# In the first batch, a layer-one tile is copied out of PSUM behind its own last matmul

## The chip, the cores and the metric

The kernel runs on one core of one Trainium2 chip. The metric is the device time of one execution in microseconds (us). Before the change it is 1329.47 us, the median of three runs (1329.26 to 1331.39).

## The reference, cut to what matters

```python
# q, k, v: (8 batches, 8 heads, 576 rows, 64); tau: a scalar
scores = (q @ k.T) / sqrt(64)
keep   = scores >= max(scores, axis=-1) - tau
attn   = exp(scores - max) where keep, else 0;  attn /= sum(attn) + 1e-9
x = (attn @ v) with heads side by side            # (4608 tokens, 512)
h = x @ w_in                                      # (4608, 2048)   "layer one"
out = (0.5 * h * (1 + erf(h / sqrt(2)))) @ w_out  # exact GELU, then "layer two": (4608, 512)
```

All of it is float32. The two weight matrices arrive as 64-bit floats and are turned into float32 on the chip, in pieces of 512 columns (lines L199 and L200 on ScalarE, L207 and L208 on VectorE, L219 on GpSimd).

## The kernel before, in words

The order of the instructions is written out by hand: each engine runs its queue in the order in which the Python code emits it. No scheduler moves anything.

**Slots.** The main loop at the end of the function runs over slots `n`. A slot is one chunk of 128 score rows of one pair of heads (for the last 64 rows of both heads together, the tail chunk). The first batch, `early`, is slots 0 to 19: chunks 0 and 1 of the four pairs in slots 0 to 7, then chunks 2, 3 and tail of each pair in turn in slots 8 to 19. `BATCH` is 20, the first slot of the second batch.

**One early slot** emits, in this order:

1. `scores`: matmuls into the PSUM tiles `sc` (L403; two buffers), and `softmax_head`: the negated row maximum `nmx` on VectorE (L415), a threshold on GpSimd (L418), and the exponential `p` on ScalarE (L420).
2. `gelus(0)`: every finished layer-one tile still in the list `late` is copied out of PSUM by ScalarE (`g<-hT`, L641). In the first batch the GELU itself is put off (`hold`), so that the ScalarE table of the exponential stays loaded. The eight copies wait in the list `held` until `gelus_held()` at slot 20.
3. In every third slot, `weigh_v`: the weights times v into a PSUM tile `xT` (L574), copied out by ScalarE (L592).
4. In the slots with a long transposed part, the first half of the weight conversion on ScalarE (L199, L200).
5. `fill`: matmuls of layer one of block 0 (L674), six or seven calls in a slot, from slot 10 on. Eight calls (two groups of four) make one tile `hT`, so that 64 calls make the eight tiles of the block. One call shows as two rows in the trace.
6. `turn_p_early`: PE transposes of the previous slot's `p` into PSUM tiles `tr` (L347), copied out by ScalarE (`pT<-tr`, L354, L357, L362, L366).
7. `softmax_tail`: VectorE masks `p` and sums it (L436). This is the last reader of `sc`.
8. The rest of the weight conversion (L199 and L200 on ScalarE, L207 and L208 on VectorE; L219 on GpSimd follows in the next slot).

**PSUM.** `hT`, `tr`, `xT` and a few others share one pool with the tag `mm` and four buffers. A new tile takes the buffer that was given back longest ago in program order, and its first matmul waits until the last reader of the old tile is done.

**SBUF scratch.** The copies `g` and the conversion's scratch `power` share a pool of ten buffers.

**Names that follow.** T1 to T8 are the eight layer-one tiles of block 0. Counting six or seven calls a slot from slot 10, the last matmul of T1 is the first call of slot 11's fill, that of T2 the third of slot 12's, T3 the fourth of slot 13's, T4 the sixth and last of slot 14's, T5 the first of slot 16's, T6 the third of slot 17's, T7 the fourth of slot 18's, T8 the sixth and last of slot 19's.

From slot 20 on, `lag[0]` is set anew in every slot (2, at the very end 0), so that the value in the diff is used in the first batch alone.

Of the kernel before, what the change touches and what calls it, by code (L numbers as in the profile page):

```python
# [18 lines left out]
def kernel(  # L19
# [606 lines left out]
    BLK_NS = N_DF * (N_DM * NS_IN + TOK // P * NS_OUT)  # L626

    late = []
    lag = [1]
    dirty = [False]  # L630
    held = []
    hold = [True]
# [665 lines left out]
```

## Time and profile before

| | us |
|---|---|
| median of three runs | 1329.47 |
| the profiled execution, its own time | 1329.71 |
| its span, first to last instruction | 1327.7 |
| PE busy in the span | 1315.7 |
| DVE, POOL, ACT busy | 1040.3, 637.1, 604.9 |

PE is TensorE's matmul queue, PEld its weight loads, DVE VectorE, ACT ScalarE, POOL GpSimd. Times in the timeline count from the start of the span. A timeline row gives start, duration, engine, line, operation, output and inputs, how many instructions are merged, and in brackets how long the engine had been idle and what released it. The slots that matter here begin with these scores (L403) on PE:

| slot | 11 | 12 | 13 | 14 | 15 | 16 | 17 | 18 | 19 | 20 |
|---|---|---|---|---|---|---|---|---|---|---|
| scores start, us | 62.4 | 68.2 | 77.4 | 82.7 | 87.5 | 96.3 | 101.5 | 106.7 | 115.3 | 121.0 |
| fill starts, us | 64.4 | 73.0 | 78.3 | 83.9 | 92.3 | 97.1 | 102.6 | 111.3 | 116.2 | none |
| transposes start, us | 66.9 | 75.9 | 80.9 | 86.3 | 95.2 | 99.7 | 105.5 | 113.7 | 118.8 | none |

### The profile page before, as it was taken

The page shows a single profiled execution, that of the slowest core. Times are in us where ns is not written, and L with a number is a line of the kernel's source. Part 1 is how long each engine was busy: PE and PEld are TensorE (multiplying, and loading weights), DVE is VectorE, ACT ScalarE, POOL GpSimd, SP SyncE. Part 2 cuts the span into 40 slices and gives each one's busy share as a digit, 9 for nine tenths or more (in the row PEclk, how much of TensorE's full clock was granted, in tenths as well). Part 3 has the DMA queues.
Part 4 walks back from the last instruction along what each step waited for, and adds up shares of the span by engine and source line. Part 5 has one row for each costly group of instructions (what it writes and reads, how often), then busy time and mean ns, then how long its engine had stood idle before and what let it go on. Part 6 is the DMA issues. An engine that isn't in the chain of part 4 may idle for free.

```text
span 1327.7 us, 19863 instructions
## 1 busy us (share of the span) xinstructions
PE 1315.7 (99%) x6306; PEld 889.1 (67%) x6306; DVE 1040.3 (78%) x2001; ACT 604.9 (46%) x1027; POOL 637.1 (48%) x1058
## 2 busy tenths in 40 slices
PE   9999999999999999999999999999999999999998
PEld 6776466576476466466466466578778787877877
DVE  6887877888888888888888888883857698386674
ACT  7988366376376368358458438232111203211120
POOL 3565545455555555655555541236264403645430
PEclk9999999999999999999999999999999999999999
DMA  7553667777776787787787775400000140000003
GB/s 250 180 177 89 143 156 164 168 161 161 190 167 157 191 185 160 191 194 164 185 202 159 177 172 110 105 9 1 1 0 1 40 107 14 0 1 0 1 0 80
DMA packets 213687, 153.14 MB, mean 115 GB/s; under 512 B 117264, under 2 KB 196992, under 8 KB 213584
## 3 DMA queue, kind: packets, MB, share of 16 engines
q1 hardware_dynamic: 195440, 125.31, 40.6%
q0 software_dynamic: 17712, 26.26, 7.4%
q8 instruction: 52, 0.85, 0.3%
q14 instruction: 51, 0.42, 0.1%
q10 hardware_dynamic: 432, 0.30, 0.1%
HBM read 56.62 MB, written 12.58 MB: 52 GB/s over the span
## 4 chain that ended last, share of the span: by engine, by line
PE 92%; ACT 2%; DVE 2%; DMA 1%; issue 1%; POOL 1%; SPq 0%; DVEq 0%; POOLq 0%; ACTq 0%
PE bank L862 34%; PE o_ps L689 17%; PE hT L674 16%; PE sc L403 13%; PE xT L574 11%; ACT p L420 1%; DVE nmx L415 1%; DMA inv<-turned 0%; PE tr L347 0%; ACT pT L354 0%; DVE p L436 0%; DVE power L208 0%; DVE power L207 0%; DMA xall<-in_moe_w_out_dram 0%; DMA turned_p<-in_moe_w_out_dram 0%
## 5 line engine op out<-in xcount | busy, mean ns | idle before, releaser
L420 ACT ACTIVATE p<-sc,nmx 128x576 f32<-128x576 f32 x288 | 202.0, 738 | 277.9 <-DVE nmx L415 277.6
L436 DVE SCALAR_TENSOR_TENSOR p<-sc,thr,p 128x576 f32<-128x576 f32 x288 | 225.4, 816 | 72.7 <-ACT p L420 65.2
L418 POOL TENSOR_SCALAR thr<-nmx,tau_eff 128x1 f32<-128x1 f32 x288 | 84.7, 296 | 335.1 <-DVE nmx L415 332.5
L674 PE MATMUL hT<-xall,w_in 128*128 128x256 f32 x1024 | 241.8, 385 | 0.0
L415 DVE TENSOR_REDUCE nmx<-sc 128x1 f32<-128x576 f32 x288 | 205.2, 749 | 44.3 <-PE sc L403 43.0
L689 PE MATMUL o_ps<-w_out,g 128*128 128x512 f32 x512 | 236.7, 602 | 0.0
L674 PEld LDWEIGHTS hT<-xall,w_in 128*128 128x128 f32 x1024 | 189.4, 190 | 51.3 <-issue 24.5
L744 DVE TENSOR_TENSOR o<-o,bank 128x256 f32<-128x256 f32 (+1 forms) x242 | 100.0, 417 | 94.5 <-PE bank L862 89.5
L744 DVE TENSOR_TENSOR c<-c,bank 128x320 f32<-128x320 f32 x304 | 146.7, 487 | 34.3 <-PE bank L862 21.1
L689 PEld LDWEIGHTS o_ps<-w_out,g 128*128 128x128 f32 x512 | 93.1, 190 | 109.6 <-issue 106.8
L403 PE MATMUL sc<-kT,qT 64*128 64x288 f32 x960 | 161.3, 429 | 2.1 <-DVE p L436 1.2
L574 PE MATMUL xT<-pT,v 128*64 128x320 f32 (+1 forms) x1240 | 159.3, 409 | 0.2
L535 DVE STREAM_TRANSPOSE turned_p<-p 128x1152 f32<-128x1152 f32 x112 | 154.4, 1378 | 3.9
L403 PEld LDWEIGHTS sc<-kT,qT 64*128 64x128 f32 x960 | 91.8, 186 | 77.0 <-issue 61.9
L574 PEld LDWEIGHTS xT<-pT,v 128*64 128x64 f32 x1240 | 86.4, 137 | 70.9 <-issue 10.4
L862 PE MATMUL bank<-w_out,c 128*128 128x256 f32 (+1 forms) x484 | 120.5, 379 | 0.8 <-DVE o L744 0.8
L260 POOL DMA_DIRECT2D v<-in_v_dram x208 | 111.2, 538 | 3.4 <-issue 1.2
L862 PEld LDWEIGHTS bank<-w_out,c 128*128 128x128 f32 x484 | 90.3, 190 | 18.9 <-DVE o L744 3.2
L929 ACT ACTIVATE c<-c 128x320 f32<-128x320 f32 (+1 forms) x80 | 46.9, 624 | 114.7 <-DVE c L744 114.6
L744 POOL TENSOR_TENSOR c<-c,g 128x320 f32<-128x320 f32 (+1 forms) x40 | 50.6, 1273 | 67.4 <-DVE c L744 67.4
L862 PE MATMUL bank<-t_out,g 128*128 128x256 f32 (+1 forms) x324 | 82.4, 377 | 0.4 <-DVE o L744 0.4
L862 PE MATMUL bank<-t_out,c 128*128 128x256 f32 x320 | 82.8, 381 | 0.0
(185 smaller groups left out, 1749.1 us busy)
## 6 DMA issues: line engine op xcount, KB each, us to landing
pT<-turned_p SPq DMA_DIRECT2D x448, 160.0 KB, 3.6
pT<-pd_tail SPq DMA_DIRECT2D x112, 80.0 KB, 3.0
q<-in_q_dram POOLq DMA_DIRECT2D x104, 72.0 KB, 3.6
k<-in_k_dram POOLq DMA_DIRECT2D x104, 72.0 KB, 3.2
inv<-turned SPq DMA_DIRECT2D x54, 128.0 KB, 4.0
v<-in_v_dram POOLq DMA_DIRECT2D x156, 40.0 KB, 3.1
out_dram<-o SPq DMA_DIRECT2D x40, 128.0 KB, 2.4
xall<-in_moe_w_out_dram SPq DMA_DIRECT2D x9, 512.0 KB, 4.9
```

Source lines behind the costliest of these rows:

```text
L260: eng.dma_start(t[r:P:4, e, 0:n, :], rows[:, r * KR:r * KR + n, :])
L403: nc.tensor.matmul(sc[e][:, h, 0:HALF], lhsT=lhsT, rhs=s["kT"][rows, at:at + HALF], start=True, stop=True)
L415: nc.vector.tensor_reduce(nmx[:, e:e + 1], sc, axis=AXIS.XY, op=ALU.max, negate=True)
L418: nc.gpsimd.tensor_scalar(thr[:, e:e + 1], nmx[:, e:e + 1], -1.0, tau_eff, op0=ALU.mult, op1=ALU.subtract)
L420: nc.scalar.activation(w[:, e * S:(e + 1) * S].rearrange("p (h s) -> p h s", h=2), sc, AF.Exp, bias=nmx[:, e:e + 1], scale=1.0)
L436: nc.vector.scalar_tensor_tensor(row, sc[e][:, :, 0:HALF], thr[:, e:e + 1], row, op0=ALU.is_ge, op1=ALU.mult, accum_out=den[e])
L535: nc.vector.transpose(turned_p[:, :, i // 2, 0:NB, i % 2 * Q:(i % 2 + 1) * Q], w.rearrange("p (e b i) -> p e b i", e=2, i=Q))
L574: nc.tensor.matmul(to, lhsT=s["v"][:, e, c, :], rhs=rhs, start=(c == 0), stop=(c == KR - 1))
L674: nc.tensor.matmul(hT[:, j % 2, :], lhsT=w_in_sb[c][:, j * P:(j + 1) * P], rhs=x_blk[n][:, c, :], start=(c == 0), stop=(c == N_DM - 1))
L689: nc.tensor.matmul(o[:, 0:d_model], lhsT=g[j][:, m * P:(m + 1) * P], rhs=w_out_sb[j], start=(j == 0), stop=(j == N_DF - 1))
L744: eng.tensor_tensor(out, a, b, op=ALU.add)
L862: nc.tensor.matmul(to, lhsT=l, rhs=r, start=start and k == 0, stop=k == len(pairs) - 1, skip_group_check=not start)
```

## The change

`lag[0]` is how many finished layer-one tiles `gelus` leaves in `late` when it is called from inside `block_steps`, right behind the last matmul of a tile. With 1, a finished tile stays in PSUM until the next one is finished or until the next slot calls `gelus(0)`. With 0, its ScalarE copy is emitted at once: ahead of the same slot's transposes and their copies.

```diff
@@ -626,7 +626,7 @@
     late = []
-    lag = [1]
+    lag = [0]
     dirty = [False]
```

In the built program the instructions of PE, DVE, POOL and SP stand in the same order as before. On ACT the eight `g<-hT` copies stand earlier, each by one slot or less; nothing else moves. The tiles' buffers turn over in another order with it.

## The prediction

> **What bounds the kernel now.** I read the chain of work that ended last first, then the busy times by stretch, then the waits inside the first batch, then its timeline. The chain:
>
> ```profile
> PE 92%; ACT 2%; DVE 2%; DMA 1%; issue 1%; POOL 1%; SPq 0%; DVEq 0%; POOLq 0%; ACTq 0%
> ```
>
> PE carries the end, so only what moves PE counts. Busy time by stretch, slots 10 to 20 (57 to 127 us) and after them; the columns are the length, then PE, PEld, DVE, ACT, POOL busy:
>
> ```profile
> 57.00:127.00 70.00, 67.82 (x372) 48.72 (x372) 57.36 (x113) 58.95 (x119) 40.04 (x59) 1.00 0.49 144
> 127.00:179.00 52.00, 51.92 (x198) 27.08 (x198) 41.50 (x78) 19.68 (x34) 28.47 (x57) 1.00 0.65 145
> ```
>
> In the first batch PE has 2.2 us of gaps, ACT is at 84%, DVE at 82%: three engines hand work round. Afterwards PE has no gap to speak of, so a shift of PE at 127 us should go through to the end. The waits from 57 to 127 us (sum, times, longest):
>
> ```profile
> ACT pT L354 <- PE tr L347: 5.7, 5, 1.6
> DVE nmx L415 <- PE sc L403: 5.4, 4, 2.2
> ...
> PEld tr L347 <- ACT pT L354: 2.4, 5, 0.5
> ...
> PE sc L403 <- DVE p L436: 0.7, 2, 0.5
> ...
> PEld tr L347 <- ACT g L641: 0.3, 1, 0.3
> ```
>
> PE's own wait is that of the transposes for a PSUM buffer: 2.4 + 0.3 us. Slot 12 shows one (timeline):
>
> ```profile
> 72.97 2.89 PEld L674 LDWEIGHTS hT<-xall,w_in 128*128 128x128 f32 x14 [0.49 <-issue]
> ...
> 72.99 0.58 ACT L641 COPY g<-hT 128x512 f32<-128x512 f32 x1
> ...
> 75.89 1.01 PEld L347 LDWEIGHTS tr<-ident,p 128*128 128x128 f32 x8
> ...
> 76.79 1.07 ACT L354 COPY pT<-tr 128x512 f32<-128x512 f32 x2 [0.54 <-PE tr L347]
> 77.43 0.14 PEld L347 LDWEIGHTS tr<-ident,p 128*128 128x128 f32 x1 [0.53 <-ACT pT L354]
> ...
> 77.60 1.14 PE L403 MATMUL sc<-kT,q_tail 128*128 128x288 f32 x4
> ```
>
> Eight transposes run, the ninth waits 0.53 us until ACT has emptied the first `tr` tile: of the four buffers a finished tile (T2) and the one in work (T3) hold two.
>
> **What the Trainium skill says.** "PSUM — Partial Sum Buffer", section "Engine vs sequencer instructions": ScalarE's queue is strict FIFO. The trace agrees: T1's last matmul is in slot 11's fill, begun at 64.4 us, yet its copy runs at 72.99, behind the exponentials that stand before it. "Perfetto Trace Analysis", "Optimization Strategy": consistent bubbles can mean that there isn't enough PSUM for the next tile. It agrees: 0.53, 0.48, 0.47 and 0.53 us at the same ninth transpose in slots 12, 13, 16, 18. "SBUF — State Buffer", "SBUF: two separate sides": a DVE operation with two SBUF inputs and a GpSimd one lock each other out. It agrees: L208 took 1.65 us at 81.60, beside L219, and 0.69 us elsewhere.
>
> **The change part by part.** Eight copies of 0.578 us (L641) move on ACT. None is added or removed, no DMA moves, and the other queues keep their order.
>
> *Buffers.* With T(k) out early, the third transpose tile gets the buffer of that tile; the built program's waits name its copy instead of the first `pT` copy. In slot 12, T2 is done by about 74.5 us (third of seven calls at 0.43 us). ACT, without T1's copy, ends its conversion at about 76.0 to 76.2, so T2's copy ends by 76.5 to 76.75, before the ninth transpose is due (76.90). The bubble goes. Its worth: from the first transpose to the next scores slot 12 takes 77.60 - 75.89 = 1.71 us, slot 15, which has no bubble, 96.36 - 95.16 = 1.20. That is **0.51 us**. Slot 18 likewise: 115.45 - 113.73 - 1.20 = **0.52 us**. Slot 19 has 14 transposes and a bubble of 0.37 us (at 120.28): 121.03 - 118.80 = 2.23 us against 1.20 + 5 x 0.126 = 1.83: **0.40 us**.
>
> *Bubbles that give nothing.* Slots 13, 16, 17 (0.48, 0.47, and 0.30 behind a `g` copy) lose theirs too, but the next full scores wait for DVE: slot 15's second score tile starts at 88.24, when L436 (87.31 + 0.81 = 88.12) frees it. That goes back without a gap over L415 (84.74), L208 and L207 (83.67, released by ACT L199), L362, to the L354 copies at 81.80, which wait for the first transpose tile, ahead of the bubble at 82.43. So these 1.25 us turn into a longer wait for DVE. I take 0; at most 1.25. In slots 12 and 18 it differs: DVE is idle 1.31 and 1.57 us before the tail chunk's L415, waiting for PE's scores, and follows PE.
>
> *ACT.* Each copy stands ahead of the `pT` copies; behind it wait these, the conversion, DVE's L207, L208 and L415, and PE through buffers. Most slots swap one copy for another. Slot 11 gains one with no idle time before L357: L199 is 0.58 us later, L207 about 0.37. The cover is DVE's 1.31 us at 78.77; without it, up to 0.58. Slot 16 gains one inside ACT's 1.48 us before L354: 0. Slot 15 loses one: 0. T4 and T8 are last in their fills; T4's copy stands where T3's stood, behind exponentials that end at 86.93, when the fill is over (86.72): 0. T8's copy can hold slot 19's L354 back by some 0.15 us; that stays behind PE, whose fifth transpose tile waits for L354: 0, at most 0.15.
>
> *Slot 20.*
>
> ```profile
> 123.10 1.41 ACT L420 ACTIVATE p<-sc,nmx 128x576 f32<-128x576 f32 x2 [1.02 <-DVE nmx L415]
> ...
> 124.40 0.58 ACT L641 COPY g<-hT 128x512 f32<-128x512 f32 x1
> ...
> 125.00 1.28 ACT L647 ACT_TABLE_LOAD   x1
> ...
> 126.29 4.27 ACT L647 ACTIVATE g<-g 128x512 f32<-128x512 f32 x8
> ...
> 131.98 1.36 ACT L420 ACTIVATE p<-sc,nmx 128x576 f32<-128x576 f32 x2
> 132.81 0.82 DVE L436 SCALAR_TENSOR_TENSOR p<-sc,thr,p 128x576 f32<-128x576 f32 x1 [2.90 <-ACT p L420]
> ...
> 134.10 1.62 PE L403 MATMUL sc<-kT,qT 64*128 64x288 f32 x8
> ```
>
> Without T8's copy the table load follows the exponentials at 124.51, not 125.00: **0.49 us** for ACT, and for DVE, idle 2.90 us for it. PE has room to follow: its next three stretched scores took 1.62, 1.79 and 1.99 us against 1.24 in an unhindered slot, 1.68 us of waiting for DVE. I take 0.49; at least 0, at most 0.58.
>
> *Scratch pool.* Ten buffers hold `g` and `power`. Each copy and each L199 now waits for another L219; by the timeline the tightest (slot 17's second L199, at 102.86, for an L219 that ended at 98.69) has 4.2 us to spare: 0.
>
> *Unknown.* Shifted by 0.5 us, an L208 may meet or miss an L219: 1.65 - 0.69 = 0.96 us either way. I take 0.
>
> *Sum:* 0.51 + 0.52 + 0.40 + 0.49 = 1.92 us. Against the profiled execution (1329.71 us, 2.0 beside its span) that is 1327.8; it was 0.24 over the median, so **1327.6 us**, 0.14% less. What a measurement can tell from no change is about 0.2%, 2.66 us: below 1326.8 is faster, above 1332.1 slower.
>
> **The rivals.**
>
> *All bubbles pay.* If slots 13, 16 and 17 count as well: 1.92 + 1.25 = 3.17 us, 1326.3 us. For it: conversion on DVE could get ahead with ACT. Against: the gapless chain above.
>
> *PE's gain is taken back.* Bubbles just become waits for DVE in slots 15, 18 and 21; only slot 20's 0.49 or nothing stays: 1329.0 us. For it: DVE at 82%. Against: its idle time before L415.
>
> *ACT becomes the bound.* A copy ahead of the `pT` copies delays pT, conversion, L415, L436 and the scores in every slot, and the time is not won back at its old place: 8 x 0.578 = 4.6 us, **1334.1 us**. It decides where ACT's idle time ahead of the `pT` copies is under 0.58 us. For it: slots 11, 14 and 17 have none, slot 12 has 0.54. Against: 14, 17 and 12 lose a copy in the same slot; 13, 16 and 19 have 1.02 to 1.48 us.
>
> *Nothing happens*, since the next slot's call empties the list anyway: the built program shows eight moved copies; counted with the second.
>
> **How the numbers follow.** Likeliest case 0.50 (own range 1326.4 to 1328.8: 1.92 us with 0.96 either way and the ends above), all bubbles 0.19, taken back 0.12, ACT the bound 0.19. Faster by over 0.2%: 0.19 and 0.08 of the first case. Slower: 0.16 of the ACT case, the rest of it small. Same: 0.57. The range, 1325.5 to 1331.5, takes in the fast rival with the spread of the runs and the milder ACT cases; left out are some 0.17.
>
> **What would show it.** Right: no idle entry at the ninth transpose in slots 12, 13, 16, 18; L641 at about 67.7, 76, 80, 86.5, 98.5, 105, 112.5 and 118.3 us; slot 20's scores at 119.6 us (121.03 before); slot 15's scores still waiting for L436, longer; ACT's table load near 123.1; from 150 us every row about 1.9 us earlier. Wrong: slot 13's or 19's scores not earlier, PE waits for `g` (L641) in place of those for L354, or a shift that changes after 180 us.

## The result, and the profile after

The changed kernel takes 1328.62 us (median of 22 runs, 1327.58 to 1329.80). The kernel before, on the same chip, takes 1330.22 us (22 runs, 1329.13 to 1332.19). The ratio is 0.9988, with a 95% interval of 0.9982 to 0.9993: 0.12% faster, 1.6 us. The interval leaves out a ratio of 1, so the gain is real, but its size lies inside the band of 0.2% that the prediction had set.

The profiled executions show where it comes from, once one thing is set aside. In the profile of the changed kernel everything from 7 us to slot 12 stands 1.01 us late: slot 0's transposes of the tail rows (L327 on PEld) start at 6.62 us before and at 7.63 after, ahead of anything that the change touches. So the spans (1327.7 and 1326.7) differ by 1.0 us only. I measure a stretch inside each profile instead, on PEld, from which the table of starts ahead of the prediction was read too: from slot 10's scores (57.20 before, 58.21 after) to the full scores at 154.66 before, 153.85 after. It took 97.46 us and takes 95.64, **1.82 us less**. The forecast was 1.92.

The chain that ended last has more PE in it than before:

```profile
PE 94%; DVE 2%; ACT 1%; issue 1%; DMA 0%; POOL 0%; DVEq 0%; POOLq 0%; ACTq 0%
```

The busy times by stretch (length, then PE, PEld, DVE, ACT, POOL) are of little use here, since they take in the shift of the start: a change of 2 us in a queue's waits hardly shows in them.

```profile
57.00:127.00 70.00, 67.75 (x379) 49.43 (x378) 58.71 (x115) 60.46 (x124) 40.48 (x62) 1.00 0.50 149
127.00:179.00 52.00, 51.97 (x201) 27.14 (x200) 41.78 (x77) 19.57 (x34) 28.82 (x58) 1.00 0.66 149
```

The waits of the changed kernel from 57 to 127 us (sum, times, longest) do show it:

```profile
DVE nmx L415 <- PE sc L403: 4.0, 4, 1.8
ACT pT L354 <- PE tr L347: 3.3, 5, 1.0
...
ACT g L641 <- PE hT L674: 2.3, 3, 1.1
PE sc L403 <- DVE p L436: 1.7, 3, 0.7
```

The waits of the transposes for L354 and for L641 (2.4 and 0.3 us) are gone from the list. In their place ACT waits 2.3 us for the end of three tiles, which costs nothing, and PE's wait for L436 grows from 0.7 to 1.7 us. Slot 12 in the timeline of the changed kernel:

```profile
76.77 0.59 ACT L641 COPY g<-hT 128x512 f32<-128x512 f32 x1
76.89 1.13 PEld L347 LDWEIGHTS tr<-ident,p 128*128 128x128 f32 x9
...
77.80 1.07 ACT L354 COPY pT<-tr 128x512 f32<-128x512 f32 x2 [0.44 <-PE tr L347]
...
78.09 1.14 PE L403 MATMUL sc<-kT,q_tail 128*128 128x288 f32 x4
```

The nine transposes are one row now; T2's copy, at 76.77, is out of the way before the ninth. L354 has not moved: 77.80 - 1.01 = 76.79, its old place. So it is the other buffer, and not an earlier L354, that lets the ninth through. From the first transpose to the next scores it is 78.09 - 76.89 = 1.20 us, where it was 1.71. Slots 20 to 22, again in the timeline of the changed kernel:

```profile
122.67 1.41 ACT L420 ACTIVATE p<-sc,nmx 128x576 f32<-128x576 f32 x2 [0.71 <-DVE nmx L415]
...
124.09 1.28 ACT L647 ACT_TABLE_LOAD   x1
...
131.08 1.35 ACT L420 ACTIVATE p<-sc,nmx 128x576 f32<-128x576 f32 x2
...
131.90 0.82 DVE L436 SCALAR_TENSOR_TENSOR p<-sc,thr,p 128x576 f32<-128x576 f32 x1 [2.41 <-ACT p L420]
...
133.59 1.24 PE L403 MATMUL sc<-kT,qT 64*128 64x288 f32 x8
...
134.86 1.42 DVE L415 TENSOR_REDUCE nmx<-sc 128x1 f32<-128x576 f32 x2
```

The table load follows the exponentials at once, and the scores at 133.59 run through in 1.24 us, where they took 1.62.

### The profile page after: what moved, and what is told of

Same layout as the page of the kernel before. It is cut to its first block, busy times and chain, and to the rows that moved or that the text cites. A ratio compares the mean times of both kernels' runs of the same rounds, so it can differ in the third digit from the quotient of the medians.

```text
span 1326.7 us, 19869 instructions
## 1 busy us (share of the span) xinstructions
PE 1315.1 (99%) x6306; PEld 889.7 (67%) x6306; DVE 1040.7 (78%) x2001; ACT 604.2 (46%) x1027; POOL 634.7 (48%) x1058
## 4 chain that ended last, share of the span: by engine, by line
PE 94%; DVE 2%; ACT 1%; issue 1%; DMA 0%; POOL 0%; DVEq 0%; POOLq 0%; ACTq 0%
PE bank L862 34%; PE o_ps L689 17%; PE hT L674 17%; PE sc L403 14%; PE xT L574 12%; DVE nmx L415 1%; ACT p L420 1%; DVE p L436 1%; DVE power L208 1%; PE tr L347 1%; DVE power L207 0%; DMA turned_p<-in_moe_w_out_dram 0%; PE tr L317 0%; ACT pT L354 0%; PE idle L147 0%
## 5 line engine op out<-in xcount | busy, mean ns | idle before, releaser
L420 ACT ACTIVATE p<-sc,nmx 128x576 f32<-128x576 f32 x288 | 201.9, 738 | 276.7 <-DVE nmx L415 276.4
L436 DVE SCALAR_TENSOR_TENSOR p<-sc,thr,p 128x576 f32<-128x576 f32 x288 | 225.4, 816 | 71.8 <-ACT p L420 64.5
L415 DVE TENSOR_REDUCE nmx<-sc 128x1 f32<-128x576 f32 x288 | 205.3, 750 | 43.1 <-PE sc L403 41.8
L574 PE MATMUL xT<-pT,v 128*64 128x320 f32 (+1 forms) x1240 | 159.4, 409 | 0.2
L574 PEld LDWEIGHTS xT<-pT,v 128*64 128x64 f32 x1240 | 86.3, 137 | 70.9 <-issue 10.8
```

The lines of the kernel that those rows point to most:

```text
L415: nc.vector.tensor_reduce(nmx[:, e:e + 1], sc, axis=AXIS.XY, op=ALU.max, negate=True)
L420: nc.scalar.activation(w[:, e * S:(e + 1) * S].rearrange("p (h s) -> p h s", h=2), sc, AF.Exp, bias=nmx[:, e:e + 1], scale=1.0)
L436: nc.vector.scalar_tensor_tensor(row, sc[e][:, :, 0:HALF], thr[:, e:e + 1], row, op0=ALU.is_ge, op1=ALU.mult, accum_out=den[e])
L574: nc.tensor.matmul(to, lhsT=s["v"][:, e, c, :], rhs=rhs, start=(c == 0), stop=(c == KR - 1))
```

## The experiments

The theory: PE's transposes stop for PSUM buffers; only those stops count after which DVE waits for PE (slots 12, 18, 19), while the others turn into a wait for DVE; and slot 20 gains because ACT's queue is one copy shorter. The rivals are those of the prediction. Each gain below is of the stretch from slot 10's scores to the full scores near 154 us, in one profile; two profiles agree in it, slot by slot where nothing differs, to some 0.05 us, far finer than the runs do. "Less than before" is against 97.46 us, "than the changed kernel" against 95.64.

**Which copies matter.** Four kernels made from the one before, in which chosen slots alone use 0 for `lag[0]`:

```diff
         gelus(0)
+        if early:
+            lag[0] = 0 if n in (19,) else 1      # T8 alone
+            # T2 and T7: (12, 18); T3 and T5: (13, 16); all but T8: range(19)
```

T8 alone. 

> The kernel before, with T8 alone copied out behind its last matmul (slot 19); T1 to T7 one tile later as before. The measure is the PE shift: the time from slot 10's scores (L403, 57.20 us before) to the full scores at 154.66 us, 97.46 us in the kernel before and 95.64 in the changed one, 1.82 less. If slot 19's bubble (0.40) and slot 20's shorter ACT queue (0.4) each pay on their own, the stretch is 0.8 us shorter: some 0.06% of the time. If the gain needs all eight copies, or lies in the buffers of the earlier slots, it is under 0.2 us. If only the queue in slot 20 pays, 0.4.

Measured: 154.46 - 57.80 = 96.66 us, 0.80 less. Of it 0.39 come in slot 19 and 0.38 between slots 20 and 23. Runs: 1329.85 against 1330.12 us, ratio 0.9998 (0.9989 to 1.0006); that interval can't tell 0.06%. Both places pay, each on its own.

T2 and T7 alone. 

> The kernel before, with T2 and T7 alone copied out behind their last matmuls (slots 12 and 18, the slots with the long PE work). If those two bubbles reach the end because DVE waits for PE there, the stretch from slot 10's scores to the scores at 154.66 us is 1.03 us shorter (0.51 and 0.52): 0.08% of the time. If PE's gain is taken back by DVE, it is unchanged.

Measured: 154.40 - 57.98 = 96.42 us, 1.04 less. Runs: 1328.98 us, ratio 0.9992 (0.9984 to 1.0001). As the theory has it; PE's gain is not taken back there.

T3 and T5 alone. 

> The kernel before, with T3 and T5 alone copied out behind their last matmuls (slots 13 and 16). Their bubbles at the ninth transpose (0.48 and 0.47 us) and the one of 0.30 us behind T5's copy in slot 17 should go. If the next slot but one waits for DVE anyway, the stretch from slot 10's scores to the scores at 154.66 us does not change (under 0.1 us) and the wait of the scores for L436 in slots 15 and 18 grows by about as much. If all bubbles pay, it is 1.25 us shorter. If ACT is the bound, it is longer, by up to 0.58 us a copy.

Measured: 155.32 - 57.92 = 97.40 us, 0.06 less. Runs: 1330.15 us, ratio 0.9999 (0.9991 to 1.0008). The bubbles did go: the transposes of this kernel have no wait for L641, and 1.4 us of waits for L354 where there were 2.4. What they turned into stands in PE's timeline of slot 15, first before, then in this kernel:

```profile
87.53 1.94 PE L403 MATMUL sc<-pd_tail,qT 64*128 64x288 f32 x8 [0.27 <-DVE p L436]
```

```profile
88.22 1.94 PE L403 MATMUL sc<-pd_tail,qT 64*128 64x288 f32 x8 [0.69 <-DVE p L436]
```

PE arrives 0.46 us earlier and waits 0.42 longer. The rivals "all bubbles pay" (1.25 us) and "ACT becomes the bound" (longer) are out.

All but T8. 

> The changed kernel, with T8 alone still copied in slot 20 as before. If the four terms add up, the stretch from slot 10's scores to the scores at 154.66 us is 1.03 us shorter than before and 0.8 us longer than in the changed kernel: a time some 0.08% under that of before. If the early copies only pay together, it is shorter by less than 0.5 us.

Measured: 154.23 - 57.83 = 96.40 us, 1.06 less, as with T2 and T7 alone. Runs: 1328.77 us, ratio 0.9993 (0.9985 to 1.0001). T1, T3 to T6 add nothing, and the parts add up: 0.80 + 1.04 + 0.06 = 1.90 against 1.82 for all.

**Slot 20's queue.** The changed kernel with a copy put back where T8's stood:

```diff
         if n == BATCH:
+            t8 = held[-1][2]
+            nc.scalar.copy(t8, t8)
             gelus_held()
```

> The changed kernel, with one more ScalarE copy of the size of T8's (from T8's SBUF tile onto itself) in slot 20, where T8's copy stood before: ahead of the table load for the GELU. It leaves slot 19 as it is and gives slot 20's queue its 0.58 us back. If slot 20's part of the gain is ACT's queue there, the stretch grows by 0.39 us (the measured share of slot 20), from 95.64 to about 96.0, all of it between the scores at 125 and those at 138 us. If slot 20's part came from the buffer or from slot 19, it stays at 95.64.

Measured: 154.09 - 58.07 = 96.02 us, 0.38 more than the changed kernel, all of it between slots 20 and 23. Runs: 1328.99 us, ratio to before 0.9989 (0.9981 to 0.9998). ACT's timeline:

```profile
122.49 1.41 ACT L420 ACTIVATE p<-sc,nmx 128x576 f32<-128x576 f32 x2 [0.71 <-DVE nmx L415]
123.80 0.61 ACT L1160 COPY g<-g 128x512 f32<-128x512 f32 x1
124.42 1.28 ACT L647 ACT_TABLE_LOAD   x1
```

Slot 19 is untouched here, and the copy put back costs the 0.38 us that slot 20 had gained: slot 20's share is ACT's queue.

**Is it DVE that takes the other bubbles back?** A conversion step costs ACT a L199 and a L200, DVE a L207 and a L208. `STEPS` says how many each slot does. Moving a step out of slot 13 or 16 takes it from the queues of both ahead of slot 14's or 17's maximum (L415). The changed kernel with one step moved from 16 to 18:

```diff
-    STEPS = [0, 1, 1, 1, 1, 1, 2, 1, 2, 2, 2, 2, 3, 2, 2, 3, 2, 2, 1, 0, 1]
+    STEPS = [0, 1, 1, 1, 1, 1, 2, 1, 2, 2, 2, 2, 3, 2, 2, 3, 1, 2, 2, 0, 1]
```

> The changed kernel, with one step of the weight conversion (L199, L200, L207, L208) moved from slot 16 to slot 18. In the changed kernel PE gains 0.46 us at slot 16's bubble and gives it back in slot 18, where the scores wait for DVE. If DVE's chain of L208, L415 and L436 is what takes it back, slot 17's L415 comes some 1 to 1.5 us earlier, and the bubbles of slots 16 and 17 now pay: the scores of slot 18 start 0.5 to 0.75 us earlier and the stretch from slot 10's scores to the scores at 154.66 us, 95.64 in the changed kernel, becomes 94.9 to 95.2. Slot 18 has 1.57 us of idle DVE for the moved 1.1 us. If something else takes the gain back, or DVE is late in slot 19 instead, it stays at 95.6 or more.

Measured: 152.14 - 57.05 = 95.09 us, 0.55 less than the changed kernel. Runs: 1328.09 us, ratio to before 0.9984 (0.9977 to 0.9990). The same edit of `STEPS` on the kernel before:

> The kernel before (every copy one tile later), with the same step of the conversion moved from slot 16 to slot 18 as in the run on the changed kernel. It tells how much of that run's gain is due to the conversion alone. With the bubbles of 0.47 and 0.30 us in slots 16 and 17 still there, PE reaches slot 18's scores at about the time that DVE freed them, so that only the 0.1 to 0.2 us of that wait can go: the stretch of 97.46 us becomes 97.2 to 97.4. If the conversion alone is the gain, it becomes 96.7.

Measured: 154.80 - 57.83 = 96.97 us, 0.49 less than before. Runs: 1329.95 us, ratio 0.9996 (0.9987 to 1.0004). This expectation missed. PE's timeline of slots 17 and 18 says why, first before, then in this kernel:

```profile
105.75 0.99 PE L347 MATMUL tr<-ident,p 128*128 128x128 f32 x5
106.67 1.81 PE L403 MATMUL sc<-pd_tail,qT 64*128 64x288 f32 x8
```

```profile
106.40 0.71 PE L347 MATMUL tr<-ident,p 128*128 128x128 f32 x5
107.04 1.58 PE L403 MATMUL sc<-pd_tail,qT 64*128 64x288 f32 x8
```

The fifth transpose no longer waits: with the step gone from slot 16, slot 17's maximum and exponentials come earlier, and T5's copy behind them (105.47 us, where it was 105.78 in a profile that started 0.6 us sooner). So slot 17's 0.30 us go with 0.2 us of waiting for DVE. So this pair doesn't separate bubble and conversion. Slot 13 does. The changed kernel with a step moved from 13 to 18:

```diff
-    STEPS = [0, 1, 1, 1, 1, 1, 2, 1, 2, 2, 2, 2, 3, 2, 2, 3, 2, 2, 1, 0, 1]
+    STEPS = [0, 1, 1, 1, 1, 1, 2, 1, 2, 2, 2, 2, 3, 1, 2, 3, 2, 2, 2, 0, 1]
```

> The changed kernel, with one step of the conversion moved from slot 13 to slot 18. If DVE is what takes back slot 13's bubble, slot 15's scores do not wait for L436 any more and come 0.45 us earlier; slots 16 to 18 follow, and the stretch is 95.2 us against 95.64. If not, 95.6.

Measured: 151.75 - 57.05 = 94.70 us, 0.94 less than the changed kernel and 2.76 less than before. Runs: 1326.70 us, ratio to before 0.9971 (0.9959 to 0.9983): the lowest median here, of six runs. And the same edit of `STEPS` on the kernel before:

> The kernel before (every copy one tile later) with one conversion step moved from slot 13 to slot 18. On the changed kernel this step won 0.94 us. If that is DVE's wait in slot 15 plus slot 13's bubble, 0.46 us of it need the early copy, and here the gain is about 0.5 us: the stretch of 97.46 us becomes about 97.0. If the move of the step is worth the same whatever the copies do, it becomes 96.5. If slot 18 takes all of it back, 97.4.

Measured: 153.80 - 56.98 = 96.82 us, 0.64 less than before, between the two forecasts. Runs: 1329.32 us, ratio 0.9995 (0.9987 to 1.0003). From slot 12's transposes to slot 15's L574 the changed kernel with the step moved has gained 1.77 us, the kernel before with the step moved 0.93. The 0.84 between them are T2's 0.51 and 0.33 more. With the step in slot 13, that slot's bubble was worth 0.02 to 0.05. PE's timeline of slot 15, first in the kernel before with the step moved, then in the changed kernel with the step moved, and slot 18 of the latter:

```profile
86.96 1.36 PE L403 MATMUL sc<-pd_tail,qT 64*128 64x288 f32 x8
```

```profile
86.07 1.48 PE L403 MATMUL sc<-pd_tail,qT 64*128 64x288 f32 x8
...
104.90 1.94 PE L403 MATMUL sc<-pd_tail,qT 64*128 64x288 f32 x8 [0.83 <-DVE p L436]
```

There is no wait for DVE ahead of slot 15's scores any more. Between their two tiles some is left: they take 1.36 and 1.48 us, against 1.24 unhindered. The 0.12 between the two and the 0.33 make up slot 13's 0.46. Slot 18 has a wait of 0.83 us: part of the gain is given back there.

So it is shown that the conversion step, which stands ahead of L415 in DVE's queue, takes the bubble back. Which engine's share of the step does it is not: the step is L207 and L208 on DVE and also L199 and L200 on ACT, and DVE's second L207 in slot 13 waits for ACT's L199 (0.42 us before, 0.19 in the changed kernel). The runs move both together.

**Both steps.** To keep that part of the gain too, the second step went from 16 to 19, or both went to 18. Each is the changed kernel with this edit:

```diff
-    STEPS = [0, 1, 1, 1, 1, 1, 2, 1, 2, 2, 2, 2, 3, 2, 2, 3, 2, 2, 1, 0, 1]
+    STEPS = [0, 1, 1, 1, 1, 1, 2, 1, 2, 2, 2, 2, 3, 1, 2, 3, 1, 2, 2, 1, 1]
```

> The changed kernel, with one conversion step moved from slot 13 to slot 18 and one from slot 16 to slot 19. With only the first, PE kept slot 13's bubble (slot 15's scores 1.24 us earlier than in the changed kernel, from the same slot 10) and gave 0.76 us back at slot 18's scores. With both, DVE should not be late there, so that 0.5 to 0.76 us more stay; against it, ACT gets 1.15 us of conversion in slot 19 with some 0.7 us idle, which can hold slot 20's exponentials back by 0.45 us. The stretch from slot 10's scores to the scores at 154.66 us: 94.71 with the first alone, 94.0 to 94.6 with both. If DVE is not what takes the gain back at slot 18, it is 94.7 or more.

Measured: 152.25 - 57.57 = 94.68 us, the same as with the first step alone. Runs: 1327.22 us, ratio 0.9977 (0.9967 to 0.9987). Slot 18 gives back 0.26 instead of 0.76 us, but 0.43 are lost in slot 20, where the conversion stands before the exponentials in ACT's timeline:

```profile
119.91 0.68 ACT L199 ACTIVATE power<-xall 128x512 f32<-128x512 f32 x1
120.50 0.66 ACT L200 ACTIVATE w_out<-xall 128x512 uint32<-128x512 uint32 x1
121.19 1.37 ACT L420 ACTIVATE p<-sc,nmx 128x576 f32<-128x576 f32 x2
```

```diff
-    STEPS = [0, 1, 1, 1, 1, 1, 2, 1, 2, 2, 2, 2, 3, 2, 2, 3, 2, 2, 1, 0, 1]
+    STEPS = [0, 1, 1, 1, 1, 1, 2, 1, 2, 2, 2, 2, 3, 1, 2, 3, 1, 2, 3, 0, 1]
```

> The same with both steps moved to slot 18, so that slot 19 is left alone. Slot 18 then has 2.2 us more of L207 and L208 on DVE with 1.57 us of idle time: slot 19's L415 can be late by some 0.6 us, and slot 20's scores with it. The stretch is 94.0 us where the work of slot 18 is hidden, 94.6 where the 0.6 us come through.

Measured: 153.55 - 57.45 = 96.10 us, worse than the changed kernel by 0.46. Runs: 1328.60 us, ratio 0.9988 (0.9981 to 0.9994). Neither forecast held; ACT's timeline shows the wait:

```profile
116.67 0.68 ACT L199 ACTIVATE power<-xall 128x512 f32<-128x512 f32 x1 [2.21 <-POOL w_out L219]
...
117.81 0.74 ACT L420 ACTIVATE p<-sc,nmx 128x576 f32<-128x576 f32 x1
```

L199 waits 2.21 us for an L219 of GpSimd: by the order of the code, seven `g` tiles and three conversions in flight then hold all ten scratch buffers. That is the pool which the prediction had looked at and found with 4.2 us to spare; a third step in one slot uses that up.

## Why the prediction was right, point by point

| step of the sum | forecast, us | measured, us |
|---|---|---|
| slot 12's bubble | 0.51 | 0.51 |
| slot 18's bubble | 0.52 | 0.52 |
| slot 19's bubble | 0.40 | 0.39 |
| slots 13, 16, 17, with 0.01 ahead of slot 12 | 0, at most 1.25 | 0.02 |
| slot 20, T8's copy out of ACT's queue | 0.49 | 0.38 |
| sum | 1.92 | 1.82 |

The measured column is the change of PE's shift against before: at slot 12's transposes it is +1.00 us (75.89 to 76.89), at slot 13's fill +0.49; at slot 15's transposes +0.47; at slot 18's +0.48, at slot 19's fill -0.04; at slot 20's scores -0.43; at 154 us -0.81.

*Buffers.* The ninth transpose no longer waits for L354, as it must if it takes the finished tile's buffer, and T2's copy came at 76.77, which is 75.76 without the late start; the forecast was about 76. The other copies stand at 68.56, 81.04, 87.30, 99.44, 106.25, 113.81 and 119.22, within 0.3 us of the list when 1.01 is taken off. The strict order of ScalarE's queue, on which this rests (the Trainium skill, "PSUM — Partial Sum Buffer", section "Engine vs sequencer instructions"), shows best in the kernel with both steps in slot 18: there slot 19's maximum (L415) ends at 115.87 us, but the exponential that needs it (L420) starts at 117.81, behind L200 and the L199 that waits for GpSimd until 116.67.

*Bubbles that give nothing.* Right, and by the mechanism named: slot 15's scores wait 0.71 us for L436, not 0.27. The chain behind that L436 runs over ACT as well as DVE, as the prediction's own list of it says.

*Slot 20.* The mechanism was right, the size was not: this term was 0.11 us too large. ACT, and with it L436, did come 0.47 us earlier against PE's shift (131.90 is 0.90 before its old place, the score matmuls of slot 21 0.43). But slot 22's maximum (L415, at 134.86) then waits for its scores, which stand behind the layer-two matmuls in PE's queue (these end at 133.65): L415 is 0.85 earlier and L436 after it 0.81. What the prediction took for room, 1.68 us of waiting in three scores, was room for PE to follow DVE; it missed that DVE in turn follows PE after the first of them.

*ACT.* Covered as said. Slot 11's extra copy made L199 0.32 us later, not 0.58, and L207 0.04, not 0.37; DVE's 1.31 us of idle time in slot 13 took it.

*The lock between DVE and GpSimd.* The long instruction moved by one and the sum hardly changed: in slot 13 L207 takes 1.57 us and L208 0.69, together 2.26, where it was 0.42 and 1.65, together 2.07. The wait for L199 behind them is shorter by as much (0.19 us, not 0.42). The 0.96 us either way did not appear.

*The forecast of 1327.6 us* was made against a median of 1329.47 us from three runs; the same kernel gave 1330.22 in 22. So the absolute figure is 1.0 us under the measured 1328.62, of which 0.75 come from the three runs. The measured difference of 1.6 us and the profile's 1.82 agree within the interval of the ratio (0.9 to 2.4 us).

*The shift after 180 us.* The prediction named a change there as a sign of being wrong, and there is one. The changed kernel keeps its 0.80 to 0.82 us ahead of the kernel before from 155 to 683 us; at the scores of 689.51 (before) and 688.45 (after) it is 1.06, and at the last matmul still 1.03. Nothing ties these 0.24 us to the change: near 680 us GpSimd waits for a DMA (L622), 0.6 us before and 0.4 after, and the threshold behind it, for which DVE's L436 waits, comes earlier by as much. The kernel with T3 and T5 alone, which gains 0.06 us in the first batch, gains 0.25 us at the same scores.

*Rivals.* "All bubbles pay" fell with the T3 and T5 kernel (0.06 us instead of 1.25), "PE's gain is taken back" with the T2 and T7 kernel (1.04 instead of 0), "ACT becomes the bound" with both.

## What to carry to other kernels

In this case a bubble on the busiest engine was worth its length only where the engine that needs the result next was waiting for it: 0.5 us removed ahead of a DVE that was idle for 1.3 us paid in full, and 0.46 us removed where DVE's next result hung on a chain that starts ahead of the bubble paid 0.02. When a buffer pool stalls, look first for the tile that is finished and still sits in it, and give it back before asking for another buffer. After such a change, look at the engine that now makes the first one wait: moving one step of its work by five slots won another 0.94 us, until the next shared thing, a scratch pool or a queue, ran out.

## What I had not expected of the hardware

The first microseconds differ from profile to profile by up to 1.25 us, two thirds of the effect. Slot 0's transposes of the tail rows (L327) start between 6.38 us (the changed kernel with a step moved from 13 to 18) and 7.63 us (the changed kernel) in the thirteen profiles. Late loads are not the reason: where they start latest, the row names no DMA as what released them. The transposes ahead of them (L317) begin at 4.16 or 4.17 us in all thirteen, and what differs is how long these take. The latest L327 on PEld, then the L317 on PE of the two kernels, in the order in which they were named:

```profile
7.63 0.20 PEld L327 LDWEIGHTS tr<-ident,q 64*64 64x64 f32 x4 [0.17 <-issue]
```

```profile
5.31 1.14 PE L317 MATMUL tr<-ident,k 128*64 128x128 f32 x15
```

```profile
6.14 1.55 PE L317 MATMUL tr<-ident,k 128*64 128x128 f32 x15
```

The same fifteen transposes take 1.14 us in one and 1.55 in the other. The profile gives the granted clock as 1.00 in both from 4 to 6.6 us, so the cause stays open. In ten of the thirteen profiles slot 10's scores follow L327 by 50.57 to 50.60 us, in the other three by 50.46 to 50.67.

Nor is a shift kept to the end. In the kernel with all copies but T8's early, PE waits for a DMA far behind the first batch, where the kernel before does not wait:

```profile
673.57 2.34 PE L574 MATMUL xT<-pT,v 128*64 128x256 f32 x18 [0.84 <-DMA pT<-pd_tail]
```

Ahead of it this kernel is 0.43 us earlier than the kernel before (scores at 668.22 and 668.65), behind it 1.02 us later (676.90 and 675.88). So for changes of one or two us a stretch inside the profile, which begins after the first loads and ends ahead of such waits, tells more than the time of the run.
